# One table for the order of all steps up to the second mixture pass, the borders between the passes included

## Chip, cores and metric

The kernel runs on one core of a Trainium2 chip. The metric is device microseconds of that core from launch to end; smaller is better. A time is the median of several runs, and one run is also recorded by the hardware profiler.

## What is computed

Three layers follow each other on 2304 tokens (4 batches of 576), all in 32-bit floats. The layout calls (transposes and reshapes between the layers) are cut here:

```python
def phi(x):                       # q, k: [4, 8, 576, 64], w_phi: [64, 128]
    proj = x @ w_phi
    proj = proj - max(abs(proj), axis=-1)
    return concat(exp(proj), exp(-proj))
kv, z = phi(k).T @ v, sum(phi(k))
x = (phi(q) @ kv) / (phi(q) @ z + 1e-6)          # attention, to [2304, 512]

h = maximum(x @ moe_w_in, 0)                     # [512, 2048]
x = (h * h) @ moe_w_out                          # squared-relu MLP

p = probs / (probs.sum(-1) + 1e-9)               # mixture of 4 experts
out = sum(p[:, e] * (maximum(x @ w1[e], 0) @ w2[e]) for e in range(4))
```

## The kernel before

Every large product is made three times over with operands split into a high and a low part (`split`, L78 makes the high part with a copy on ScalarE, L83 the low part with a subtraction on VectorE or GpSimd), so that the reduced-precision matmuls add up to a 32-bit result. TensorE therefore does far more matmul time than any other engine does work.

The work has four stages.

- **Attention and half of the MLP.** Sixteen objects `Pair(b, c)`, one per batch b and pair of heads c, each load q, k and v, transpose them (`t_pe`, L203), split them (`t_hi`, `t_lo`), project them (`project`, L231 to L233), subtract the row maximum (`shift`: a reduction L239 into `mx` and a subtraction L243 into `pm`), take exponentials (`exp_k`, L256, into `kf`; `q_pe` L264 and `q_exp` L273 into `q`), multiply keys by values (`kv_pe`, L279 and L284, with `va` the values), multiply queries by that (`num_pe`, L302, with `z` the result of `kv_pe`), divide and transpose back. Batches 0 and 1 go at once into the MLP (`Unit`: `hidden` L451, `relu`, `square`, `g_hi`, `g_lo`, `out` L497, `add` L505), whose 16 weight blocks (`Matrix`) are read here as 64-bit numbers and narrowed to 32 bits in several VectorE and ScalarE steps (`widen`, L392, takes two bit masks; then `widen_power` to `widen_mul`) and stored for later.
- **MLP of batches 2 and 3** (L1128 onward): 8 groups of two weight blocks. The two batches are multiplied together in a Strassen-like scheme: `PairUnit.product` (L1029) makes seven products of six matmuls each into four accumulators `px`, `py`, `pz`, `pv`, and `PairUnit.add` (L1039) adds them into `u` on VectorE. The operands of the products (`Operands`) are B11, T2, T1, T3, B22, B21 and T4, quarters of the activations or sums of them (`f`), each with a high part `oh` and a low part `ol`. The last 64 rows of each batch are carried apart (`RestUnit.hidden`, 24 matmuls, L1059, with the operand `rest`). `Act` makes relu, square (L995, L997) and the split `gh`, `gl`; the second matmul is `MlpOut.mm` (L1082) with `MlpOut.add` (L1089).
- **Mixture of batches 0 and 1**: 16 groups of 42 product matmuls and 48 output matmuls (`MixOut.mm`, L1104, with `MixOut.add`, L1113).
- **Mixture of batches 2 and 3 and of the rest rows**: 16 groups, with `RestUnit` again.

Between two stages lies a border: the operands of the next stage are made from sums that the stage before is still finishing, and weights of the next stage are loaded, summed (`Weights.sums`, GpSimd, L932, into `f`) and split.

What runs when is an order written by hand. Each engine executes its instructions in program order, and the DMA queue of SyncE issues loads and stores in program order. The program is the list `plan`, sorted by a number. The function `at` gives each step that number: for the early part of the program, as a place out of the table `PLACES`, and after that, as a time that the formulas in `plan_tail` and its helpers work out from fixed offsets (`plan_weights`, `plan_pair`, `plan_out`, `plan_operands`):

```python
def at(t, fn, *args):
    if t < UNTIL:
        x = getattr(fn, "__self__", None)
        t = UNTIL * next(places["" if x is None else type(x).__name__, fn.__name__]) / STEPS
    plan.append((t, len(plan), fn, args))
```

Before, `UNTIL` is 485.0, and the table holds 1519 places, the attention stage and the first border. The second border (MLP to mixture) and the third (mixture to mixture with rest rows) come from the formulas.

Of the kernel before, what the change touches and what calls it, by code (L numbers as in the profile page):

```python
# [21 lines left out]
def fused_kernel(  # L22
# [484 lines left out]
    def new_x2(b):  # L507
# [12 lines left out]
            5, 8, 28,  # L520
        ),
        ("", "load_wd"): (
            1,
        ),
        ("", "split"): (
            7,
        ),
        ("Pair", "lqk"): (
            0, 12, 4, 13, 14, 29, 65, 72, 40, 104, 95, 96, 141, 117, 132, 157, 183, 218, 193, 211, 223, 285,
            300, 264, 342, 344, 308, 382, 375, 446, 451, 475, 484, 573, 549, 566, 503, 572, 529, 706, 749, 800,  # L530
            826, 924, 868, 927, 1092, 1034,
        ),
        ("Pair", "lv"): (
            18, 24, 23, 38, 33, 61, 37, 130, 133, 116, 112, 91, 152, 240, 174, 214, 187, 269, 301, 216, 338,
            362, 328, 390, 404, 318, 351, 402, 568, 464, 571, 461, 651, 643, 526, 745, 587, 825, 702, 969, 982,
            818, 1024, 771, 801, 947, 893, 1064,
        ),
        ("Pair", "t_pe"): (
            2, 6, 20, 26, 48, 41, 85, 75, 100, 127, 155, 134, 161, 171, 184, 232, 246, 216, 257, 293, 275, 311,
            340, 326, 387, 359, 410, 430, 471, 497, 534, 548, 531, 602, 654, 687, 715, 762, 780, 876, 897, 908,  # L540
            951, 962, 1008, 1009, 1072, 1105,
        ),
        ("Pair", "t_hi"): (
            3, 9, 21, 27, 54, 49, 89, 78, 114, 138, 162, 151, 173, 186, 207, 233, 254, 229, 266, 302, 278, 323,
            345, 337, 393, 388, 425, 455, 476, 510, 540, 575, 537, 607, 655, 711, 748, 768, 787, 896, 906, 920,
            955, 963, 1010, 1028, 1081, 1116,
        ),
        ("Pair", "t_lo"): (
            10, 15, 25, 36, 55, 53, 97, 90, 122, 143, 165, 154, 178, 190, 210, 241, 255, 237, 271, 310, 303,
            327, 347, 341, 395, 400, 427, 459, 487, 518, 551, 579, 557, 614, 670, 714, 750, 786, 806, 899, 932,  # L550
            948, 956, 981, 1011, 1051, 1088, 1131,
        ),
        ("Pair", "project"): (
            16, 22, 34, 51, 56, 63, 102, 99, 124, 145, 169, 170, 197, 206, 222, 249, 265, 272, 289, 313, 324,
            343, 354, 360, 405, 403, 429, 465, 506, 533, 556, 592, 623, 650, 689, 740, 778, 802, 851, 911, 944,
            959, 975, 1003, 1060, 1100, 1143, 1170,
        ),
        ("Pair", "shift"): (
            17, 30, 44, 57, 71, 79, 107, 105, 139, 149, 172, 180, 200, 225, 230, 261, 268, 283, 305, 315, 329,
            350, 358, 380, 414, 407, 443, 481, 521, 543, 588, 604, 635, 677, 707, 752, 790, 809, 862, 917, 945,  # L560
            971, 994, 1047, 1074, 1113, 1158, 1183,
        ),
        ("Pair", "exp_k"): (
            42, 32, 47, 68, 81, 84, 131, 118, 140, 179, 199, 189, 219, 227, 248, 270, 273, 297, 312, 316, 330,
            367, 368, 391, 437, 440, 457, 536, 542, 558, 615, 657, 671, 696, 712, 764, 850, 833, 869, 931, 993,
            1002, 1059, 1083, 1093, 1160, 1165, 1200,
        ),
        ("Pair", "q_pe"): (
            35, 39, 58, 64, 82, 94, 126, 119, 142, 175, 196, 198, 220, 253, 245, 286, 277, 291, 331, 320, 348,
            370, 369, 389, 428, 424, 478, 514, 581, 584, 613, 669, 675, 743, 804, 777, 835, 881, 936, 968, 990,  # L570
            1043, 1032, 1066, 1087, 1147, 1182, 1219,
        ),
        ("Pair", "q_exp"): (
            46, 50, 70, 73, 86, 111, 137, 125, 150, 182, 202, 203, 221, 262, 256, 292, 290, 299, 333, 321, 357,
            377, 383, 413, 436, 450, 483, 523, 595, 596, 634, 701, 679, 755, 836, 779, 855, 889, 939, 970, 1006,
            1044, 1041, 1068, 1115, 1180, 1189, 1223,
        ),
# [3 lines left out]
        ("Pair", "z_out"): (  # L581
            59, 93, 156, 217, 259, 307, 353, 406, 460, 587, 705, 828, 902, 1037, 1111, 1237,
        ),
        ("Pair", "num_pe"): (
            60, 74, 108, 115, 160, 176, 224, 236, 279, 267, 334, 314, 356, 376, 418, 438, 470, 490, 598, 617,
            710, 717, 839, 837, 921, 973, 1045, 1049, 1135, 1120, 1246, 1242,
        ),
        ("Pair", "den"): (
            69, 77, 113, 120, 164, 188, 228, 238, 287, 276, 335, 322, 409, 379, 419, 448, 499, 493, 599, 629,
            724, 725, 858, 848, 954, 986, 1055, 1050, 1138, 1126, 1260, 1247,  # L590
        ),
        ("Pair", "divide"): (
            83, 80, 146, 144, 208, 191, 239, 247, 295, 294, 349, 336, 411, 394, 421, 449, 504, 507, 608, 632,
            736, 731, 859, 853, 966, 991, 1061, 1057, 1145, 1139, 1261, 1251,
        ),
        ("Pair", "xt_pe"): (
            109, 153, 226, 258, 306, 355, 415, 462, 508, 641, 753, 860, 992, 1063, 1150, 1274,
        ),
        ("Pair", "x_hi"): (
            121, 163, 244, 274, 309, 361, 416, 472,  # L600
        ),
        ("Pair", "x_lo"): (
            129, 166, 250, 281, 317, 365, 417, 477,
        ),
        ("Pair", "x_rest"): (
            128, 159, 235, 263, 319, 378, 422, 463, 513, 649, 763, 879, 998, 1096, 1168, 1282,
        ),
        ("Pair", "put_rest"): (
            204, 234, 260, 346, 381, 445, 432, 625, 515, 703, 842, 1076, 1151, 1319, 1265, 1309,
        ),  # L610
        ("Pair", "x_out"): (
            527, 648, 757, 884, 1001, 1071, 1169, 1278,
        ),
        ("Pair", "put_x"): (
            726, 658, 840, 976, 1015, 1272, 1245, 1286,
        ),
        ("Matrix", "load"): (
            11, 31, 135, 106, 282, 384, 325, 442, 528, 576, 453, 662, 603, 735, 694, 751, 794, 852, 827, 886,
            957, 999, 907, 1082, 1102, 1128, 1058, 1192, 1175, 1238, 1204, 1254,
        ),  # L620
# [12 lines left out]
        ("Matrix", "widen_add"): (
            67, 103, 231, 213, 433, 435, 371, 524, 597, 656, 546, 719, 645, 773, 747, 814, 843, 903, 874, 952,
            995, 1035, 978, 1099, 1134, 1162, 1124, 1222, 1194, 1257, 1243, 1308,
        ),
        ("Matrix", "widen_sign"): (
            76, 123, 243, 252, 401, 447, 373, 525, 577, 653, 561, 722, 647, 775, 734, 824, 831, 887, 873, 949,
            1005, 1039, 961, 1090, 1133, 1176, 1107, 1224, 1201, 1270, 1234, 1304,
        ),  # L640
        ("Matrix", "widen_mul"): (
            87, 147, 280, 284, 468, 454, 386, 554, 605, 666, 590, 737, 663, 781, 783, 841, 854, 915, 877, 958,
            1022, 1054, 1007, 1108, 1140, 1178, 1132, 1225, 1232, 1279, 1255, 1312,
        ),
        ("Matrix", "store"): (
            181, 158, 372, 408, 559, 467, 486, 578, 665, 682, 591, 738, 716, 792, 817, 846, 861, 923, 922, 984,
            1038, 1077, 1018, 1144, 1159, 1185, 1220, 1249, 1331, 1292, 1275, 1346,
        ),
        ("Matrix", "hi"): (
            110, 167, 296, 304, 496, 473, 516, 609, 636, 668, 620, 744, 676, 784, 791, 864, 882, 916, 894, 996,  # L650
            1052, 1070, 1026, 1146, 1163, 1186, 1179, 1240, 1235, 1287, 1264, 1315,
        ),
        ("Matrix", "lo"): (
            185, 194, 364, 374, 502, 489, 532, 612, 652, 690, 621, 746, 767, 796, 795, 866, 885, 930, 919, 1014,
            1053, 1078, 1027, 1149, 1174, 1187, 1198, 1244, 1262, 1291, 1271, 1338,
        ),
        ("Unit", "hidden"): (
# [4 lines left out]
        ),  # L662
        ("Unit", "relu"): (
            412, 439, 501, 488, 555, 585, 611, 639, 688, 685, 759, 733, 812, 830, 898, 871, 912, 967, 1021, 989,
            1086, 1091, 1136, 1122, 1196, 1208, 1236, 1268, 1295, 1307, 1317, 1337,
# [24 lines left out]
        ),  # L690
        ("", "open_early"): (
            1322,
        ),
        ("", "open_late"): (
            1376,
# [83 lines left out]
    UNTIL = 485.0  # L779
# [490 lines left out]
```

## Time and profile before

| quantity | value |
|---|---|
| median of 3 runs | 1392.85 us (1389.75 to 1393.58) |
| time of the profiled execution | 1391.17 us |
| its span in the trace | 1389.4 us |
| TensorE (PE) busy | 1361.9 us, 98% of the span |
| VectorE (DVE) busy | 868.8 us, 63% |
| ScalarE (ACT) busy | 511.7 us, 37% |
| GpSimd (POOL) busy | 522.3 us, 38% |
| 16 DMA engines, mean | 66 GB/s to and from HBM |
| mean granted TensorE clock | 0.998 of full speed |

Busy time is the time in which an engine has an instruction under way. The profiled execution's own time is 1.8 us longer than its span, which is what lies around the recorded instructions, and 1.7 us under the median. In the profile, PE is TensorE's matmul and PEld its weight load, which overlaps it; L12 is line 12 of the kernel; a wait names the operation that the engine waited for. The four stages differ in what waits, so stretches of time are read apart: attention runs to about 395 us, the first border to 480, the MLP's middle groups to 590, the second border to 660, the first mixture's middle groups to 935, the third border to 985, and the last stage to the end.

### The profile page before, as it was taken

The numbers are of one execution on the slowest core, as the hardware profiler recorded it, in microseconds if no ns is written. First come the engines' busy times: TensorE is split into PE (matmuls) and PEld (weight loads), VectorE is DVE, ScalarE is ACT, GpSimd is POOL, SyncE is SP. The second block draws the span as 40 slices with busy tenths as digits, with TensorE's granted clock in tenths as the row PEclk, the third lists the DMA queues.
The fourth block names the chain that finished last, engine by engine and source line by source line (L and its number), as shares of the span: only waits on it lengthen the run. The fifth ranks groups of instructions, "written<-read, shape, count | busy, mean of one in ns | idle before, by whom it ended". The sixth has DMA issues, their size and how long they took to land.

```text
span 1389.4 us, 18889 instructions
## 1 busy us (share of the span) xinstructions
PE 1361.9 (98%) x7300; PEld 1171.7 (84%) x7300; DVE 868.8 (63%) x1302; ACT 511.7 (37%) x908; POOL 522.3 (38%) x382
## 2 busy tenths in 40 slices
PE   7999999999999999999999999999999999999998
PEld 7999888889877888887888888887888888888887
DVE  5777667796785455576655655668655555555554
ACT  4655655554554432342322232234312212212311
POOL 1000111110247776567544535444543443443430
PEclk9999999999999999999999999999999999999999
DMA  5433433442342111102111121213211211110102
GB/s 145 102 89 99 105 107 98 119 117 79 121 149 76 46 31 46 32 16 76 62 58 34 61 61 31 61 31 107 75 31 31 61 31 31 61 31 31 46 1 76
DMA packets 130250, 92.57 MB, mean 67 GB/s; under 512 B 65648, under 2 KB 108784, under 8 KB 130160
## 3 DMA queue, kind: packets, MB, share of 16 engines
q1 hardware_dynamic: 128848, 89.00, 22.1%
q10 hardware_dynamic: 1312, 2.36, 0.4%
q8 instruction: 58, 0.95, 0.3%
q14 instruction: 32, 0.26, 0.1%
HBM read 75.60 MB, written 15.73 MB: 66 GB/s over the span
## 4 chain that ended last, share of the span: by engine, by line
PE 92%; DVE 4%; ACT 1%; POOL 0%; DMA 0%; issue 0%; SPq 0%; ACTq 0%; DVEq 0%; POOLq 0%
PE pa L1104 27%; PE pv L1029 7%; PE pz L1029 7%; PE pa L1082 7%; PE px L1029 7%; PE pm L497 6%; PE ph L451 6%; PE pa L1059 5%; PE py L1029 4%; PE pa L302 3%; PE pa L284 2%; PE pm L302 2%; PE pm L284 2%; PE pp L231 1%; PE pp L233 1%; PE pp L232 1%
## 5 line engine op out<-in xcount | busy, mean ns | idle before, releaser
L83 POOL TENSOR_TENSOR w<-f,w 128x1024 fp32r<-128x1024 f32 (+1 forms) x80 | 184.5, 2327 | 284.3 <-ACT w L78 284.3
L1113 DVE SCALAR_TENSOR_TENSOR x<-pa,prob,x 128x512 f32<-128x512 f32 x270 | 201.8, 750 | 131.7 <-PE pa L1104 131.6
L1104 PE MATMUL pa<-w2l,gh 128*128 128x512 f32 x576 | 224.5, 390 | 1.3 <-ACT gh L1001 0.7
L1104 PE MATMUL pa<-w2h,gl 128*128 128x512 f32 x576 | 224.3, 389 | 1.0 <-DVE gl L1007 1.0
L1104 PE MATMUL pa<-w2h,gh 128*128 128x512 f32 x576 | 224.3, 389 | 0.0
L1036 ACT ACTIVATE u<-px 128x512 f32<-128x512 f32 x40 | 24.0, 599 | 455.2 <-PE px L1029 454.9
L83 POOL TENSOR_TENSOR wl<-wf,wh 128x512 fp32r<-128x512 f32 x32 | 42.7, 1338 | 346.3 <-ACT wh L78 311.7
L83 POOL TENSOR_TENSOR w2l<-f,w2h 128x1024 fp32r<-128x1024 f32 x40 | 97.1, 2428 | 137.6 <-ACT w2h L78 137.6
L1001 ACT ACTIVATE gh<-u 128x512 fp32r<-128x512 f32 x136 | 85.7, 631 | 156.2 <-DVE u L1039 149.8
L1104 PEld LDWEIGHTS pa<-w2h,gl 128*128 128x128 f32 x576 | 108.1, 188 | 24.2 <-DVE gl L1007 1.8
L1104 PEld LDWEIGHTS pa<-w2l,gh 128*128 128x128 f32 x576 | 108.2, 188 | 24.1 <-issue 1.1
L1104 PEld LDWEIGHTS pa<-w2h,gh 128*128 128x128 f32 x576 | 108.2, 188 | 21.8
L932 POOL TENSOR_TENSOR f<-f 128x256 f32<-128x256 f32 x160 | 120.2, 772 | 10.2 <-DMA f<-w_i 6.8
L1029 PE MATMUL px<-oh,w 128*128 128x512 f32 x320 | 98.6, 389 | 0.0
L1029 PE MATMUL pz<-oh,w 128*128 128x512 f32 x320 | 98.6, 389 | 0.0
L1029 PE MATMUL pv<-oh,w 128*128 128x512 f32 x320 | 98.6, 389 | 0.0
L1007 DVE SCALAR_TENSOR_TENSOR gl<-u,gh 128x512 fp32r<-128x512 f32 x96 | 73.5, 774 | 26.9 <-ACT gh L1001 25.3
L1039 DVE TENSOR_TENSOR u<-pz,u 128x512 f32<-128x512 f32 x80 | 55.3, 691 | 51.3 <-PE pz L1029 50.5
L78 ACT ACTIVATE w<-f 128x1024 fp32r<-128x1024 f32 (+1 forms) x80 | 77.1, 1009 | 6.4 <-POOL f L932 6.4
L1039 DVE TENSOR_TENSOR u<-py,u 128x512 f32<-128x512 f32 x40 | 27.7, 691 | 80.5 <-PE py L1029 50.5
L1059 PEld LDWEIGHTS pa<-rest,w 128*128 128x128 f32 x576 | 72.2, 191 | 1.8
L1089 DVE TENSOR_TENSOR x<-pa,x 128x512 f32<-128x512 f32 (+1 forms) x84 | 49.3, 600 | 37.7 <-PE pa L1082 37.6
(145 smaller groups left out, 2969.9 us busy)
## 6 DMA issues: line engine op xcount, KB each, us to landing
f<-in_moe_w_dram SPq DMA_DIRECT2D x96, 256.0 KB
raw<-in_moe_w_in_dram SPq DMA_DIRECT2D x16, 512.0 KB
raw<-in_moe_w_out_dram SPq DMA_DIRECT2D x16, 512.0 KB
f<-in_moe_w_dram SPq DMA_DIRECT2D x64, 128.0 KB
qk<-in_q_dram SPq DMA_DIRECT2D x32, 128.0 KB
qk<-in_k_dram SPq DMA_DIRECT2D x32, 128.0 KB
va<-in_v_dram SPq DMA_DIRECT2D x32, 128.0 KB
w_o<-wf SPq DMA_DIRECT2D x16, 256.0 KB
```

The costliest lines, as they stand in the source:

```text
L78: nc.scalar.activation(out=dst, in_=src, func=AF.Copy)
L83: eng.tensor_tensor(out=dst, in0=a, in1=b, op=ALU.subtract)
L451: nc.tensor.matmul(p[:, :n], lhsT=a, rhs=m, start=i == 0, stop=i == len(ops) - 1)
L497: nc.tensor.matmul(p[:, :n], lhsT=a, rhs=m, start=i == 0, stop=i == len(ops) - 1)
L932: nc.gpsimd.tensor_tensor(out=s[:, i], in0=a, in1=b, op=op)
L1001: nc.scalar.activation(out=self.gh, in_=self.r, func=AF.Copy if self.square else AF.Relu)
L1029: nc.tensor.matmul(p, lhsT=a, rhs=m, start=start and i == 0, stop=i == len(ops) - 1, skip_group_check=not start)
L1039: nc.vector.tensor_tensor(out=self.u[out], in0=self.p[a], in1=self.u[b], op=ALU.add)
L1059: nc.tensor.matmul(q, lhsT=a[:, s, k], rhs=m[:, kk], start=kk + j == 0, stop=kk == KD - 1 and j == 2)
L1082: nc.tensor.matmul(self.p[:, :n], lhsT=a, rhs=m, start=i == 0, stop=i == len(ops) - 1)
L1104: nc.tensor.matmul(self.p, lhsT=a, rhs=m, start=i == 0, stop=i == len(ops) - 1)
L1113: nc.vector.scalar_tensor_tensor(out=o, in0=p, scalar=pe, in1=o, op0=ALU.mult, op1=ALU.add)
```

## The change

The code that makes the work is the same; every step is still there once, with the same instructions. The table `PLACES` has 2800 places in place of 1519, and `UNTIL` is 1023.0, so that the table also sets the order through the MLP pass, the first mixture pass and the first group of the second one, all three borders among it. The places in the part that had a table before are new as well. The formulas still order what comes after. Lines after the table move by 76 (L1029 becomes L1105). Cut to the entries that the text speaks of:

```diff
         ("Pair", "lv"): (
-            18, 24, 23, 38, 33, 61, 37, 130, 133, 116, 112, 91, 152, 240, 174, 214, 187, 269, 301, 216, 338,
-            362, 328, 390, 404, 318, 351, 402, 568, 464, 571, 461, 651, 643, 526, 745, 587, 825, 702, 969, 982,
-            818, 1024, 771, 801, 947, 893, 1064,
+            43, 44, 39, 84, 70, 96, 65, 34, 138, 172, 177, 194, 196, 147, 101, 203, 287, 212, 289, 310, 244, 283,
+            305, 333, 430, 387, 468, 466, 390, 460, 504, 436, 488, 505, 631, 762, 712, 824, 622, 847, 1008, 811, 842,
+            1116, 1117, 1014, 1176, 1101,
         ),
         ("Pair", "t_lo"): (
-            10, 15, 25, 36, 55, 53, 97, 90, 122, 143, 165, 154, 178, 190, 210, 241, 255, 237, 271, 310, 303,
+            7, 12, 17, 38, 47, 53, 90, 68, 95, 115, 140, 150, 156, 193, 181, 234, 229, 257, 288, 269, 303, 335, 346,
...
         ("Pair", "kv_pe"): (
-            47.25, 52, 88, 92, 140.25, 148, 215, 215.25, 248.25, 251, 297.25, 298, 339, 352, 396, 399, 457.25, 458, 568.25, 586, 671.25, 692, 764.25, 765, 888, 891, 1030, 1030.25, 1109, 1109.25, 1213, 1218,
+            46, 50, 98, 97, 139, 154, 195, 198, 247, 266, 304, 302, 347, 342, 404, 406, 475, 490, 594, 585, 670, 698,
+            786, 790, 911, 900, 1010, 1012, 1118, 1125, 1220, 1197,
         ),
...
         ("Matrix", "widen"): (
-            19, 62, 168, 195, 397, 431, 332, 491, 564, 626, 535, 697, 631, 756, 700, 808, 803, 872, 849, 933,
+            129, 27, 159, 275, 421, 414, 242, 530, 545, 643, 491, 704, 599, 749, 660, 819, 750, 895, 806, 948, 970,
...
         ("Operands", "sum"): (
-            1326, 1330, 1333, 1349,
+            1324, 1330, 1350, 1390, 1782, 1837, 1844, 1845, 2608, 2626, 2627, 2636,
         ),
...
         ("Operands", "lo"): (
-            1361, 1375, 1380, 1340, 1341, 1370, 1393,
+            1353, 1367, 1373, 1365, 1347, 1380, 1408, 1897, 1877, 1914, 1925, 1942, 1922, 1954, 2675, 2684, 2682,
+            2690, 2685, 2692, 2696,
         ),
         ("Rest", "make"): (
-            1392,
+            1392, 2631,
         ),
...
         ("RestUnit", "hidden"): (
-            1407, 1474,
+            1407, 1419, 1547, 1614, 1681, 1748, 1824, 1893, 2717, 2767,
         ),
...
+        ("MixOut", "add"): (
+            1973, 1961, 2027, 1969, 1977, 1983, 1994, 1980, 2021, 2031, 2057, 2017, 2037, 2058, 2042, 2041, 2060,
...
-    UNTIL = 485.0
+    UNTIL = 1023.0
```

Three places show what this does to the engines' order; a row with `x8` stands for eight such instructions in a row, and `x_2_4480`, `va_108` or `w_8895` are buffers with their numbers.

**Place A: TensorE in the attention stage**, where the third pair's keys times values (`kv_pe`, L279 and L284) follow its last projection (L233) and two kinds of transposes (L264 for queries, L203 for the next input). Before:

```order
L233 MATMUL pp<-wd_h,th 128x256
L264 MATMUL pa<-ident,pm 128x128 x4
L203 MATMUL pa<-ident,qk 128x128 x8
L279 MATMUL pm<-va_108,kf 128x160
L284 MATMUL pm<-va_108,kf 128x80 x8
```

With the change:

```order
L233 MATMUL pp<-wd_h,th 128x256
L264 MATMUL pa<-ident,pm 128x128 x4
L203 MATMUL pa<-ident,qk 128x128 x5
L302 MATMUL pm<-z_110,q 128x96 x8
L302 MATMUL pm<-z_110,q 128x130 x2
L264 MATMUL pa<-ident,pm 128x128 x4
L231 MATMUL pp<-wd_h,tl 128x256
L232 MATMUL pp<-wd_l,th 128x256
L233 MATMUL pp<-wd_h,th 128x256
...
L279 MATMUL pm<-va_108,kf 128x160
L284 MATMUL pm<-va_108,kf 128x80 x8
```

The second half of the previous pair's `num_pe` (L302) and a whole further projection (four times L231 to L233) now stand between the projection that the exponentials need and the matmuls that need the exponentials.

**Place B: VectorE at the first border**, around the making of `rest`, with the MLP's first groups under way (`u` are sums of accumulators, L997 a square). Before:

```order
L1039 TENSOR_TENSOR u<-py,u 128x512
L1039 TENSOR_TENSOR u<-pz,u 128x512
L83 TENSOR_TENSOR rest<-x_4_4482,rest 128x1024
L1039 TENSOR_TENSOR u<-pv,u 128x512
L1039 TENSOR_TENSOR u<-pz,u 128x512
L997 TENSOR_TENSOR u<-u 128x512 x2
```

With the change:

```order
L1115 TENSOR_TENSOR u<-py,u 128x512
L1115 TENSOR_TENSOR u<-pz,u 128x512
L83 TENSOR_TENSOR f<-x_2_4472,f 128x1024
L83 TENSOR_TENSOR rest<-x_4_4474,rest 128x1024
L1115 TENSOR_TENSOR u<-pz,u 128x512
L1115 TENSOR_TENSOR u<-pv,u 128x512
L1073 TENSOR_TENSOR u<-u 128x512 x2
```

The sum `f` (operand T4) has moved to just ahead of the low part of `rest`, and the sum from `pz` now precedes that from `pv`. On TensorE a product of the second group stands between the first group's last products, and then the first `RestUnit.hidden`.

**Place C: TensorE at the third border**, the last two products of the first group (B21 into `px`, T4 into `pv`), `RestUnit.hidden` (L1059, with `rest`) and the first output matmuls. Before:

```order
L1029 MATMUL px<-ol,w_8895 128x512
L1029 MATMUL px<-oh,w_8895 128x512 x2
...
L1029 MATMUL pv<-ol,w_8895 128x512
L1029 MATMUL pv<-oh,w_8895 128x512 x2
...
L1059 MATMUL pa<-rest,w_8895 128x256 x24
L1104 MATMUL pa<-w2l,gh 128x512
```

With the change:

```order
L1105 MATMUL px<-ol,w_8861 128x512
L1105 MATMUL px<-oh,w_8861 128x512 x2
...
L1135 MATMUL pa<-rest,w_8861 128x256 x24
L1105 MATMUL pv<-ol,w_8861 128x512
L1105 MATMUL pv<-oh,w_8861 128x512 x2
...
L1180 MATMUL pa<-w2l,gh 128x512
```

The 24 matmuls of the rest rows now stand ahead of the product with T4 in place of behind it. On POOL, ahead of these matmuls, the low parts before stood as B22, B21, then four weight sums, then T4; now the four weight sums stand between B22's low part and B21's.

## Rows read from the trace of the kernel before

**Rows 1.** The page: busy time of TensorE, and one of its costliest groups.
```profile
PE 1361.9 (98%) x7300; PEld 1171.7 (84%) x7300; DVE 868.8 (63%) x1302; ACT 511.7 (37%) x908; POOL 522.3 (38%) x382
...
L1104 PE MATMUL pa<-w2h,gh 128*128 128x512 f32 x576 | 224.3, 389 | 0.0
```

**Rows 2.** Busy time by stretch (columns in the second line; x is instructions).
```profile
core 0: us, PE busy (x) PEld busy (x) DVE busy (x) ACT busy (x) POOL busy (x), PEclk, DMA share, GB/s
0.00:25.00 25.00, 18.17 (x138) 17.22 (x139) 13.79 (x22) 10.57 (x22) 4.86 (x22) 1.00 0.58 141
25.00:395.00 370.00, 364.92 (x2507) 333.46 (x2506) 270.75 (x470) 200.20 (x458) 40.58 (x31) 1.00 0.38 105
395.00:480.00 85.00, 80.15 (x392) 66.26 (x391) 52.14 (x72) 41.72 (x64) 59.45 (x39) 1.00 0.28 90
590.00:660.00 70.00, 66.80 (x338) 56.22 (x337) 49.16 (x64) 26.41 (x39) 50.57 (x33) 1.00 0.15 46
935.00:985.00 50.00, 46.94 (x215) 37.98 (x214) 41.27 (x47) 20.35 (x26) 30.38 (x19) 1.00 0.32 103
```

**Rows 3.** Waits of TensorE from 25 to 395 us: total, times, longest.
```profile
PE pa L284 <- DMA va<-in_v_dram: 1.6, 1, 1.6
PE pa L284 <- ACT kf L256: 1.3, 1, 1.3
PE pm L284 <- ACT kf L256: 0.8, 1, 0.8
```

**Rows 4.** The same from 395 to 480 us.
```profile
PE pv L1029 <- DVE u L1039: 1.3, 1, 1.3
PE pm L497 <- DVE x L505: 1.2, 1, 1.2
```

**Rows 5.** The same from 590 to 660 us.
```profile
PE pa L1082 <- DVE x L1089: 2.2, 2, 1.7
```

**Rows 6.** The same from 935 to 985 us.
```profile
PE pv L1029 <- POOL ol L83: 1.7, 1, 1.7
PE pa L1104 <- ACT gh L1001: 0.7, 1, 0.7
```

**Rows 7.** Busy time by stretch, around a wait at 201.6 us.
```profile
203.00:207.00 4.00, 4.00 (x14) 3.24 (x13) 1.77 (x2) 0.92 (x2) 0.00 (x0) 0.58 0.45 133
```

**Rows 8.** The chain that ended last (start, duration, what).
```profile
27.46 2.23 PE pm L302 x20
...
427.90 2.34 DVE rest L83
...
968.78 2.40 POOL ol L83
...
978.11 2.87 PE pa L1059 x24
...
1371.28 13.64 PE pa L1104 x60
```

**Rows 9.** Groups of instructions of VectorE by line (busy us, mean ns).
```profile
L1039 DVE TENSOR_TENSOR u<-pz,u 128x512 f32<-128x512 f32 x80 | 55.3, 691 | 51.3 <-PE pz L1029 50.5 <-POOL f L932 0.7
...
L243 DVE TENSOR_TENSOR pm<-pp,mx 128x1024 f32<-128x1024 f32 x32 | 39.2, 1225 | 5.0 <-PE pa L264 2.2 <-ACT wh L78 0.8
L239 DVE TENSOR_REDUCE mx<-pp 128x8 f32<-128x1024 f32 x32 | 39.0, 1219 | 8.8 <-PE pp L233 8.6
...
L392 DVE TENSOR_SCALAR power<-raw 128x512 uint32<-128x512 uint32 x32 | 14.9, 465 | 0.8 <-DMA raw<-in_moe_w_in_dram 0.8
```

**Rows 10.** The same of ScalarE.
```profile
L256 ACT ACTIVATE kf<-pm 128x512 f32<-128x512 f32 x64 | 36.8, 630 | 4.8 <-DVE pm L243 4.7
```

**Rows 11.** Timeline of VectorE and of POOL at the third border (start, duration, instruction).
```profile
957.76 2.42 POOL L83 TENSOR_TENSOR w2l<-f,w2h 128x1024 fp32r<-128x1024 f32 x1 [5.96 <-ACT w2h L78]
...
958.69 2.57 DVE L83 TENSOR_TENSOR ol<-x,oh 128x1024 fp32r<-128x1024 f32 x1
...
961.84 1.21 DVE L83 TENSOR_TENSOR ol<-f,oh 128x1024 fp32r<-128x1024 f32 x1
```

More of the change, by code (lines that the diff above doesn't have):

```diff
@@ L519, in fused_kernel @@
         ("", "clear"): (
-            5, 8, 28,
+            10, 57, 30,
         ),
         ("", "load_wd"): (
-            1,
+            3,
         ),
         ("", "split"): (
-            7,
+            4,
         ),
         ("Pair", "lqk"): (
-            0, 12, 4, 13, 14, 29, 65, 72, 40, 104, 95, 96, 141, 117, 132, 157, 183, 218, 193, 211, 223, 285,
-            300, 264, 342, 344, 308, 382, 375, 446, 451, 475, 484, 573, 549, 566, 503, 572, 529, 706, 749, 800,
-            826, 924, 868, 927, 1092, 1034,
+            0, 13, 5, 6, 31, 18, 42, 48, 55, 75, 110, 74, 117, 132, 165, 207, 160, 146, 243, 256, 228, 274, 246, 293,
@@ L677, in fused_kernel @@
-            1017, 1123, 1121, 1172, 1156, 1206, 1217, 1258, 1277, 1310, 1318, 1332, 1350,
+            443, 471, 501, 528, 553, 627, 611, 662, 717, 696, 793, 744, 828, 836, 897, 898, 1013, 972, 1087, 1026,
+            1114, 1090, 1181, 1151, 1230, 1223, 1260, 1277, 1306, 1331, 1337, 1345,
         ),
         ("Unit", "out"): (
[4 rows of a table removed]
[4 rows of a table added]
         ),
         ("Unit", "add"): (
[4 rows of a table removed]
[4 rows of a table added]
         ),
         ("", "open_early"): (
-            1322,
+            1318,
         ),
         ("", "open_late"): (
-            1376,
+            1383,
@@ L720, in fused_kernel @@
+            2298, 2344, 2390, 2436, 2482, 2528, 2544, 2592, 2673, 2756, 2772,
         ),
         ("Weights", "load2"): (
-            1385, 1419, 1424,
+            1358, 1397, 1447, 1537, 1604, 1671, 1738, 1806, 1908, 1912, 1953, 2025, 2096, 2142, 2188, 2234, 2280,
+            2326, 2372, 2418, 2464, 2510, 2567, 2541, 2641, 2697, 2654,
         ),
         ("Weights", "sums"): (
-            1334, 1390, 1460,
+            1320, 1369, 1475, 1521, 1588, 1655, 1722, 1781, 1854, 1960, 1997, 2024, 2079, 2125, 2171, 2217, 2263,
@@ L726, in fused_kernel @@
+            2309, 2355, 2401, 2447, 2493, 2539, 2565, 2632, 2689, 2757,
         ),
         ("Weights", "hi"): (
-            1352, 1391, 1475,
+            1326, 1394, 1482, 1524, 1591, 1658, 1725, 1783, 1849, 1964, 1966, 2033, 2082, 2128, 2174, 2220, 2266,
+            2312, 2358, 2404, 2450, 2496, 2545, 2588, 2630, 2691, 2771,
         ),
         ("Weights", "lo"): (
-            1355, 1396, 1502,
+            1327, 1396, 1507, 1527, 1594, 1661, 1728, 1804, 1880, 1974, 1990, 2047, 2085, 2131, 2177, 2223, 2269,
@@ L732, in fused_kernel @@
+            2315, 2361, 2407, 2453, 2499, 2561, 2598, 2637, 2698, 2783,
         ),
         ("Weights", "hi_sums"): (
-            1368, 1401, 1503,
+            1354, 1384, 1515, 1530, 1597, 1664, 1731, 1789, 1855, 1981, 2003, 2029, 2088, 2134, 2180, 2226, 2272,
+            2318, 2364, 2410, 2456, 2502, 2542, 2576, 2640, 2705, 2759,
         ),
         ("Weights", "lo_sums"): (
-            1374, 1411, 1504,
+            1355, 1391, 1516, 1563, 1630, 1697, 1764, 1805, 1856, 1986, 2019, 2035, 2092, 2138, 2184, 2230, 2276,
@@ L738, in fused_kernel @@
+            2322, 2368, 2414, 2460, 2506, 2547, 2599, 2647, 2708, 2760,
         ),
         ("Weights", "hi2"): (
-            1389, 1449, 1510,
+            1377, 1449, 1485, 1553, 1620, 1687, 1754, 1807, 1915, 1985, 2030, 2062, 2108, 2154, 2200, 2246, 2292,
+            2338, 2384, 2430, 2476, 2522, 2573, 2590, 2648, 2724, 2750,
         ),
         ("Weights", "lo2"): (
-            1397, 1467, 1511,
+            1411, 1450, 1497, 1568, 1635, 1702, 1769, 1852, 1917, 2002, 2032, 2063, 2109, 2155, 2201, 2247, 2293,
@@ L775, in fused_kernel @@
-            1515, 1518, 1516, 1512, 1506, 1494, 1501,
[6 rows of a table added]
+        ),
[10 rows of a table added]
+        ),
+        ("MixOut", "add"): (
[9 rows of a table added]
         ),
```

157 lines of the change are left out of this document (79 added, 78 removed), and 87 rows, old and new, of the table PLACES.

## The prediction

> **What bounds the kernel now.** I read the page first: TensorE is busy 1361.9 of 1389.4 us [rows 1]. The change leaves every instruction in place, so the most that it can win is what TensorE doesn't use, 27.5 us, and what a wait costs beside its idle time. Then the busy time by stretch, to see where these 27.5 us lie: 6.8 in the first 25 us, 5.1 in the attention stage after that (370.00 less 364.92), 4.85 at the first border, 3.2 at the second, 3.06 at the third [rows 2]; the rest (4.5) is the end, which the change does not touch. The middle groups of the passes have no idle time at all, and the change keeps their pattern. So it is an affair of the start, of a handful of waits in attention, and of three borders. Then the waits of TensorE by stretch, to see who is late: single waits, each for another operation, the exponentials `kf` and a load of `va` in attention [rows 3], sums `u` and `x` on VectorE at the first border [rows 4], `x` at the second [rows 5], a low part `ol` on POOL and `gh` at the third [rows 6]. No engine is short over a whole stretch: in attention VectorE works 271 of 370 us, ScalarE 200; at the third border VectorE works 41 of 50 [rows 2], the tightest of all. Waits of that kind are what a better order removes: something was made too late although its engine had time before.
>
> **What a wait costs.** A matmul that ends ahead of a wait is recorded with 389 ns [rows 1], while sixty in a row take 13.64 us, 0.227 each [rows 8]. So the restart adds 0.16 us to the idle time of each wait. And once a wait costs the clock: right after the one at 201.6 us the granted clock is 0.58 for 4 us [rows 7], close to the lower level of 1.2 GHz, where the stretch as a whole shows 1.00 [rows 2], the level of 2.4. Lost there: 0.42 x 4 = 1.7 us.
>
> **The change, part by part.**
> *Attention, 25 to 395 us: 5.1.* Place A shows the pattern. The matmuls of `kv_pe` need the projection reduced, shifted and put through the exponential: 1.22 + 1.23 + 0.63 = 3.1 us [rows 9, 10]. TensorE covered that with transposes and waited 0.8 [rows 3]. With the change, the second half of a `num_pe` and a whole projection stand between. The first is 2.23 us (recorded as 20 pieces) [rows 8]; the second is 12 matmuls of 256 columns, of which 24 take 2.87 us [rows 8], so 1.43. Together 3.7 against the 0.96 us that were missing: the wait goes, with 2.7 to spare. The load of `va` that was waited for 1.6 us [rows 3] was a load of the tenth pair whose place, 568, was right ahead of its use at 568.25; now that pair's loads stand at 466, 390 and 460 and its use at 585. I take all five waits of this stretch as gone.
> *First border: 4.85, six waits.* The 1.2 us wait for `x` [rows 4] came from operand subtractions standing in a row ahead of the sums; single sums now alternate with them. Place B is where something new can be late. From the end of the product into `pz`, VectorE has a sum (0.69 [rows 9]), `f` and `rest`: with `f` at 1.21 like an uncontended operand subtraction of the same size [rows 11] and `rest` at 2.34 [rows 8] that is 4.24 us. TensorE has three products meanwhile, 18 matmuls, 4.09 us. So `RestUnit.hidden` waits 0.15 us at least; if `f` is stretched as the row of 2.57 us [rows 11] is, 1.5. I take 0.4, near the low end, because most subtractions of that size are not stretched.
> *Second border: 3.2, three waits.* Two of them are sums `x` behind the operand subtractions [rows 5]; the same cure as at the first border, with no new product ahead of its operand. I take them as gone.
> *Third border: 3.06, three waits.* Place C: the wait of 1.7 us was for the low part of T4, the last thing that POOL made [rows 6]. Now the 24 matmuls of the rest rows, 2.87 us [rows 8], run ahead of T4's product and cover it. The other two, for `gh` and for a sum, are 0.7 [rows 6] and 0.6 us, each behind an operand subtraction on VectorE that now stands elsewhere; I take them as gone. In exchange the four weight sums stand ahead of B21's low part on POOL. The sums take about as long as the hidden matmuls, one subtraction is 2.40 us [rows 8]. If the sums start late, `px` waits: between 0 and 0.9 us (the 2.87 us by which B21's low part moves back, less the 1.4 of the product and 0.6 of the sum that stood between B21's and T4's need before). I take 0.5.
> *Start: 0.6.* `widen`'s masks of the first weight block stood on VectorE ahead of the low part of the second projection's input; the masks take 0.465 us [rows 9] and about as much again for the second one, and now come behind it. Bounds: 0 (another operand is late there anyway; the 6.8 us of idle time there [rows 2] are several waits) and 0.9. I take 0.6.
> *New waits of the attention stage.* Some forty places were exchanged, and the spare time that I find at the tightest is a few tenths of a us. One short wait: 0.5, between 0 and the 1.6 of the largest one that this stage shows now [rows 3].
> *Port of SBUF.* A subtraction on VectorE of 1024 columns took 1.21 us when POOL was idle and 2.57 while POOL was in a subtraction of its own from 957.76 to 960.18 [rows 11]: it cost 1.36 more. Both borders with many operands have such pairs before and after. I take half of one more collision, 0.7; it could be none, or four.
>
> **The sum.** Idle time that goes: 5.1 + 4.85 + 3.2 + 3.06 = 16.2. Restarts: 17 waits of 0.16 = 2.8 (five, six, three and three by stretch). The clock: 1.7. Together 20.7. The start: 0.6. New: 0.4 + 0.5 + 0.5 + 0.7 + three restarts of 0.16 = 2.6. From the profiled execution's own time: 1391.17 - 20.7 - 0.6 + 2.6 = 1372.5. That execution is 1.7 us under the median of the runs; from the median it would be 1374.2. I take 1373.0.
>
> **The rivals.**
> *First, the collisions decide (1378).* The new order packs operand subtractions of VectorE and of POOL closely at borders 1 and 3. With two such collisions at each, all on the path, 4 x 1.36 = 5.4 come on top: 1378. For it speaks that VectorE is the fullest engine there; against it, that before, with as many subtractions, only the few rows named above are stretched. The Trainium skill, page "SBUF — State Buffer", section "Who interferes with whom", says that a VectorE instruction with two inputs from SBUF contends with a GpSimd instruction that reads SBUF, and that the one that comes first blocks the other wholly; by that rule every overlap costs up to a whole subtraction, and the trace's 2.57 beside 1.21 us agrees in kind.
> *Second, loads come late (1381).* In the new table five of the sixteen pairs (the second, third, fourth, fourteenth and fifteenth) have their last load of `va` within two places of its use; in the old one two had (the seventh and tenth), and one of those two waited. If all five wait as that one did, 1.6 + 0.16 each, 8.7 us come back: 1381. Against it: the place orders instructions, it doesn't time them; a load needs only its buffer, and with three buffers for `va` that is free some two pairs ahead, so it is late only if something ahead of it in the queue of SyncE waits.
> *Third, slower (1400).* The same mechanism with its other end: one store that waits for its data blocks all loads behind it in SyncE's queue. If that made every pair late by 1.74 us, 28 us would be added to 1373: 1400. It decides from the eleventh late pair on, since eleven eat the gain. Against it: DMA engines are busy 0.38 of the attention stretch [rows 2] and only one wait there is for a DMA [rows 3].
> *Fourth, nothing happens (1391).* The late operations could be late because of their own inputs, whatever the order, and each wait just turn up one instruction further on. For it speaks that no engine but TensorE is full; that is also against it, since a late operation behind idle time of its own engine would be waiting for TensorE itself, and rows 4 to 6 show VectorE and POOL instead.
>
> **How the numbers follow.** The forecast (1368 to 1376) has a chance of 0.62, the collisions 0.20, the loads 0.10, slower 0.04, nothing 0.04. A measurement of this kernel can tell about 0.3%, 4.2 us. The first three are faster by more than that: 0.92; same 0.04, slower 0.04. The range: low end without any new wait and from the fastest run, 1389.75 - 21.3 = 1368.4; high end the loads' 1381.
>
> **What the changed profile would show.** Idle time of TensorE between 25 and 985 us, now 16.2, should be under 3; no granted clock of 0.58 near 200 us. At the first border the wait before `RestUnit.hidden` (L1135) should name `rest` on VectorE and be 0.15 to 1.5 us. At the third no wait for `ol` at `pv`, and at most 0.9 us at `px`. If VectorE's `ol` and `f` rows of 1024 columns average well over 1.6 us at the borders, the first rival is right; if waits for `va` appear at several pairs, the second or third. I am wrong if waits of another kind fill the same stretches.

## The result and the profile after

The change takes 1380.16 us in the median (1379.18 to 1380.25), the kernel before, run beside it, 1391.96. The ratio is 0.9915, with a 95% interval of 0.9897 to 0.9932. That is 11.8 us faster, inside the range, but 7 us slower than the 1373.0 forecast and 4 us above the 1368 to 1376 to which the forecast gave a chance of 0.62. The profiled execution took 1380.25 us with a span of 1378.4, which stands against 1391.17 and 1389.4 before.

The busy time by stretch answers to [rows 2]; the borders lie up to 10 us earlier now, so the stretches are cut anew.

```profile
0.00:25.00 25.00, 19.40 (x141) 17.99 (x142) 14.01 (x22) 11.49 (x25) 4.80 (x22) 1.00 0.61 142
25.00:390.00 365.00, 365.00 (x2519) 334.69 (x2519) 282.98 (x478) 201.70 (x459) 44.08 (x35) 1.00 0.39 110
390.00:470.00 80.00, 76.84 (x380) 63.98 (x379) 54.64 (x64) 40.87 (x61) 55.85 (x35) 1.00 0.25 80
...
580.00:650.00 70.00, 69.05 (x348) 58.37 (x347) 49.34 (x63) 27.78 (x39) 46.97 (x32) 1.00 0.15 46
...
925.00:975.00 50.00, 48.48 (x222) 39.30 (x222) 39.91 (x46) 18.15 (x23) 26.84 (x17) 1.00 0.33 106
975.00:1378.40 403.40, 397.05 (x1912) 335.11 (x1910) 222.45 (x308) 94.40 (x132) 137.53 (x94) 1.00 0.13 40
```

Read from the first two numbers of each row: TensorE's idle time went from 6.83 to 5.60 us at the start, from 5.08 to 0 in the attention stage, from 4.85 to 3.16 at the first border, from 3.20 to 0.95 at the second, from 3.06 to 1.52 at the third. After it, where the change was expected to do nothing, it rose from 4.50 to 6.35. Together that is 9.9 us less; eleven waits fewer behind the first 25 us (six in place of 17), at 0.16 each for the restart, make it 11.7, against 11.0 in the span.

The waits of TensorE in these stretches, in the same order (first border, second, third, and 975 to 1000 us), show that none of the waits of [rows 4 to 6] is left as it was:

```profile
PE pz L1105 <- DVE x L505: 1.8, 1, 1.8
PE px L1105 <- DVE ol L83: 1.2, 1, 1.2
...
PE pz L1105 <- DVE u L1115: 1.0, 1, 1.0
...
PE pz L1105 <- DVE u L1115: 1.0, 1, 1.0
PE px L1105 <- POOL ol L83: 0.5, 1, 0.5
...
PE pa L1180 <- DVE x L1187: 1.8, 1, 1.8
```

They begin at 413.8, 417.3, 600.9, 936.4, 959.8 and 993.7 us. Five of the six are for VectorE. What it does ahead of them is in its timeline; the POOL instructions beside it are in the second group of rows (start, duration, instruction):

```profile
411.94 3.06 DVE L83 TENSOR_TENSOR ol<-x,oh 128x1024 fp32r<-128x1024 f32 x1
414.93 0.68 DVE L505 TENSOR_TENSOR x<-pm,x 128x512 f32<-128x512 f32 x1
415.53 2.80 DVE L83 TENSOR_TENSOR ol<-x,oh 128x1024 fp32r<-128x1024 f32 x1
...
595.89 3.31 DVE L83 TENSOR_TENSOR f<-x,f 128x1024 f32<-128x1024 f32 x1
...
931.53 3.26 DVE L83 TENSOR_TENSOR rest<-x,rest 128x1024 fp32r<-128x1024 f32 x1
...
990.04 4.74 DVE L1083 SCALAR_TENSOR_TENSOR gl<-u,gh 128x512 fp32r<-128x512 f32 x3
...
411.51 5.73 POOL L83 TENSOR_TENSOR w<-f,w 128x1024 fp32r<-128x1024 f32 x2 [1.17 <-ACT w L78]
...
595.65 5.26 POOL L83 TENSOR_TENSOR w<-f,w 128x1024 fp32r<-128x1024 f32 x2 [1.17 <-ACT w L78]
...
931.32 2.39 POOL L83 TENSOR_TENSOR w<-f,w 128x1024 fp32r<-128x1024 f32 x1 [6.00 <-ACT w L78]
...
988.44 2.40 POOL L83 TENSOR_TENSOR w2l<-f,w2h 128x1024 fp32r<-128x1024 f32 x1
991.81 2.42 POOL L83 TENSOR_TENSOR w<-f,w 128x1024 fp32r<-128x1024 f32 x1 [0.97 <-ACT w L78]
```

A subtraction of 1024 columns, 1.21 us when POOL is idle [rows 11], takes up to 3.31 here, and each of the four long ones lies beside a subtraction of POOL that began earlier. At 931.32 POOL begins and works to 933.71; the subtraction `rest`, which begins at 931.53, ends at 934.79, 1.08 us after POOL, so nearly all of its work was done once POOL had ended. The sum `x` at 414.93, one of whose two inputs (`pm`) lies in PSUM, keeps its 0.68 us beside the same work of POOL. Ahead of the wait at 993.7 three `gl` take 4.74 us.

The wait at 993.7 had a second price. Behind it stands this row of the busy time by stretch (the granted clock is the third number from the end):

```profile
996.00:999.00 3.00, 3.00 (x9) 2.32 (x8) 1.29 (x3) 0.00 (x0) 1.49 (x3) 0.50 0.00 0
```

Nine matmuls there were late by 1.7 us in sum against their usual distance. So this profile has no half clock at 203 us, where [rows 7] had one, and has one at 996. Whether the new order removed the one at 203 is another question (see the end).

Two theories stood against each other then. **P**: VectorE's instructions with two inputs from SBUF and GpSimd's subtractions keep each other waiting, and the new order puts them side by side. **Q**: the new order puts some steps too late by itself, and POOL has nothing to do with it. The wait names did not tell them apart.

### The profile page after: what moved, and what is told of

The parts are those of the page before. It is cut to its first block, busy times and chain, and to the rows that moved or that the text cites. A ratio compares the mean times of both kernels' runs of the same rounds, so it can differ in the third digit from the quotient of the medians.

```text
span 1378.4 us, 18841 instructions
## 1 busy us (share of the span) xinstructions
PE 1360.8 (99%) x7300; PEld 1171.7 (85%) x7300; DVE 888.4 (64%) x1302; ACT 513.9 (37%) x908; POOL 523.6 (38%) x382
## 5 line engine op out<-in xcount | busy, mean ns | idle before, releaser
L83 POOL TENSOR_TENSOR w<-f,w 128x1024 fp32r<-128x1024 f32 (+1 forms) x80 | 186.1, 2344 | 280.5 <-ACT w L78 280.5
L83 POOL TENSOR_TENSOR wl<-wf,wh 128x512 fp32r<-128x512 f32 x32 | 42.0, 1321 | 339.8 <-ACT wh L78 252.3
L83 POOL TENSOR_TENSOR w2l<-f,w2h 128x1024 fp32r<-128x1024 f32 x40 | 96.5, 2413 | 126.1 <-ACT w2h L78 126.1
L1105 PE MATMUL px<-oh,w 128*128 128x512 f32 x320 | 98.6, 389 | 0.0
L1105 PE MATMUL pv<-oh,w 128*128 128x512 f32 x320 | 98.6, 389 | 0.0
L1105 PE MATMUL pz<-oh,w 128*128 128x512 f32 x320 | 98.6, 389 | 0.0
L1083 DVE SCALAR_TENSOR_TENSOR gl<-u,gh 128x512 fp32r<-128x512 f32 x96 | 77.3, 815 | 27.3 <-ACT gh L1077 26.0
L1135 PE MATMUL pa<-rest,w 128*128 128x256 f32 x576 | 72.9, 283 | 0.0
L1115 DVE TENSOR_TENSOR u<-pv,u 128x512 f32<-128x512 f32 x80 | 55.1, 689 | 26.8 <-PE pv L1105 26.5
```

Of the source, the lines that this page charges most:

```text
L83: eng.tensor_tensor(out=dst, in0=a, in1=b, op=ALU.subtract)
L1083: nc.vector.scalar_tensor_tensor(out=self.gl, in0=self.src, scalar=0.0, in1=f32(self.gh), op0=ALU.max, op1=ALU.subtract)
L1105: nc.tensor.matmul(p, lhsT=a, rhs=m, start=start and i == 0, stop=i == len(ops) - 1, skip_group_check=not start)
L1115: nc.vector.tensor_tensor(out=self.u[out], in0=self.p[a], in1=self.u[b], op=ALU.add)
L1135: nc.tensor.matmul(q, lhsT=a[:, s, k], rhs=m[:, kk], start=kk + j == 0, stop=kk == KD - 1 and j == 2)
```

## Experiments

**Which part of the change won.** Two kernels combine the two orders: in `at`, `p` is the new table's place, `key` the pair of names that it is looked up by (the lines are shortened).

```diff
+            p = next(places[key])
-            t = UNTIL * next(places[key]) / STEPS
+            t = p - 1e6 if t < 485.0 else t                  # e1: formulas after 485
+            t = next(old[key]) - 1e6 if t < 485.0 else p - 1e5   # e2: old table first
```

> New order for the steps that had a place in the old table (attention and first border), old formulas for everything after: second and third border as before. Theory A, the rearranged second and third border gave back what they won (the trace of the change shows 5 new waits from the first border on): 1380 to 1381, the same as the change. Rival B, the second and third border each won their idle time and something else went wrong: their 3.2 + 3.06 us of idle time and six restarts of 0.16 come back, 1387.

> Old order for the steps of the old table, new order for the rest: the second and third border alone are new. Theory A: 1390 to 1392, no gain. Rival B: 1385, the 7.2 us of both borders won.

Measured: e1 1381.59 us (1380.70 to 1382.49), ratio 0.9935 with an interval of 0.9920 to 0.9949; e2 1391.49 against 1391.93 before, ratio 0.9999 (0.9987 to 1.0010). The expectation for theory A holds for e2; e1 lies 0.6 us above its 1380 to 1381. e1's profile has a half clock at 14 to 18 us that the change's has not, and from 25 us to the last matmul the two traces differ by 0.2 us. Nearly all that the change wins comes from the steps that had a table before; the second and third border in their new order are worth nothing alone. It isn't that nothing happens there. These are e2's waits of TensorE from 560 to 1050 us, in place of those of [rows 5, 6]:

```profile
PE pz L1368 <- DVE u L1378: 1.9, 2, 1.0
PE pa L1443 <- DVE x L1450: 1.9, 1, 1.9
PE px L1368 <- POOL ol L83: 0.5, 1, 0.5
```

Six waits of 6.3 us idle have become four of 4.3; the two restarts saved make it 2.3, and the half clock, which stands behind the wait for `x` here too, takes 1.7 of that.

**Without POOL's share.** Both orders were run with the low parts of the last three stages' weights left out: the matmuls read the high part in their place.

```diff
-                self.h, self.l = w1[:, 0], w1[:, 1]
+                self.h, self.l = w1[:, 0], w1[:, 0]
-            sub(nc.gpsimd, self.l[:, self.part], self.f[:, self.part], f32(self.h[:, self.part]))
+            pass
```

and likewise in `lo_sums` and `lo2`.

> The change without the GpSimd subtractions that make the low parts of the weights of the last three stages (the matmuls read the high part in their place, so the result leaves the low parts out); as many matmuls, DMAs and VectorE instructions. Theory P, VectorE's instructions with two inputs from SBUF and GpSimd's subtractions keep each other waiting, and the new waits come from that: the waits at 413, 417, 600, 936 and 993 us go (1.82, 1.16, 0.95, 0.98, 1.85 and five restarts of 0.16) and the half clock after the last (1.7): 1371 within 1.5; VectorE's 128x1024 subtractions are near 1.21 us but for those beside the weight sums. Rival Q, the new order itself puts steps too late and POOL has nothing to do with it: 1379 to 1380, the same waits.

> The same edit to the kernel before (the weights' low parts left out). Theory P: the subtractions stretched at 625 to 630 and at 950 and 959 us fall to 1.21, and of the borders' waits those at 626, 629 and 953 go, in part that at 431: 3 to 6 us, 1386 to 1389. Rival Q: 1391 to 1392.

Measured: e3 1370.03 us (1369.28 to 1370.72), ratio 0.9850 (0.9833 to 0.9866); e4 1389.09 (1387.79 to 1389.54), ratio 0.9979 (0.9969 to 0.9989). So these POOL instructions cost the new order some 10 us (1380.16 less 1370.03) and the old one 2.8 (1.5 to 4.3 by the interval), though both orders issue the same ones. The profiles of e3 and e4 have a half clock between 12 and 18 us that those of the change and of the kernel before have not. From 390 us on, where that plays no part, the last matmul comes 11.0 us sooner in e3 than in the change, and 4.5 us sooner in e4 than before. In e3 one wait is left from 390 to 1000 us, the one for POOL itself, the two subtractions at the first border are short, and so is the low part of the rest rows, by its group (busy, mean ns):

```profile
PE px L1105 <- POOL ol L83: 0.5, 1, 0.5
```
```profile
411.43 1.21 DVE L83 TENSOR_TENSOR ol<-x,oh 128x1024 fp32r<-128x1024 f32 x1
412.56 0.68 DVE L505 TENSOR_TENSOR x<-pm,x 128x512 f32<-128x512 f32 x1
413.16 1.21 DVE L83 TENSOR_TENSOR ol<-x,oh 128x1024 fp32r<-128x1024 f32 x1
```
```profile
L83 DVE TENSOR_TENSOR rest<-x,rest 128x1024 fp32r<-128x1024 f32 x2 | 2.4, 1216 | 0.0
```

Theory Q, 1379 to 1380 with the same waits, falls. What e4 says of the size, 2.8, is a little under the 3 to 6 expected, and of its waits one part was a miss: the waits of the second border at 626 and 629 us, which were to go, stay (0.62 and 1.68 us at 629 and 631 there). The 2.81 us subtraction ahead of the second stays too, now beside a low part of an operand on POOL, which e4 does not leave out.

**Is it the reading?** POOL was left with an instruction of as many columns, but one that only writes, or reads one input.

```diff
-            sub(nc.gpsimd, self.l2, self.f2, f32(self.h2))
+            nc.gpsimd.memset(f32(self.l2), 0.0)      # e7
+            copy(nc.gpsimd, self.l2, f32(self.h2))   # e8
```

> The change with the weights' low parts filled with zeros by GpSimd in place of subtracted (they are left out of the result): GpSimd writes as much and reads nothing. If the reading of two engines is what collides (theory P as the trace suggests): no VectorE subtraction beside such a fill is stretched, 1370 to 1371 as without the instruction. If any GpSimd work in SBUF beside VectorE collides: VectorE is held up for the length of a fill, about 1.0 us by the row of 128x800 at 0.77, and the time lies between, 1373 to 1378.

> The same with the low parts made by GpSimd as copies of the high parts (again left out of the result): one input in place of two. If one read of GpSimd is enough to collide: the waits of the change remain in part, 1373 to 1380 by the length of a copy. If only two reads collide: 1370 to 1371.

Measured: e7 1369.19 us, e8 1369.29, both like e3. The times alone don't answer, since a fill takes 0.96 us and a copy 1.05 where a subtraction takes 2.4, so there is less to meet. The rows do. In e7 two of VectorE's subtractions lie beside fills alone, and both keep their 1.21 us:

```profile
411.61 1.21 DVE L83 TENSOR_TENSOR ol<-x,oh 128x1024 fp32r<-128x1024 f32 x1
...
915.08 1.21 DVE L83 TENSOR_TENSOR f<-x 128x1024 f32<-128x1024 f32 x1
...
411.18 0.96 POOL L1022 MEMSET w<- 128x1024 f32 x1
...
915.22 0.96 POOL L1022 MEMSET w<- 128x1024 f32 x1 [4.75 <-PE px L1105]
```

In e8 the subtractions beside copies are stretched, by half a microsecond here, and the two copies take 2.81 together:

```profile
590.40 1.77 DVE L83 TENSOR_TENSOR f<-x 128x1024 f32<-128x1024 f32 x1
592.20 1.73 DVE L83 TENSOR_TENSOR f<-x,f 128x1024 f32<-128x1024 f32 x1
...
590.05 2.81 POOL L80 CAST w<-w 128x1024 fp32r<-128x1024 f32 x2 [1.16 <-ACT w L78]
```

So one read by GpSimd is enough, and writing is not. My expectation of e8, waits in part and 1373 to 1380, was a miss: the rows are stretched, but none of the five waits comes back, because the stretch is only as long as what POOL has left to do. Two subtractions beside fills are few cases. This is what the rule named in the prediction says: the Trainium skill, page "SBUF — State Buffer", section "Who interferes with whom", has the collision between VectorE's two inputs and a GpSimd instruction that reads, not one that only writes. Here the trace agrees, 1.21 beside fills and 1.73 to 3.41 beside reads in the rows shown here.

**Moving the POOL instructions away.** e5 changes places in the table alone; nothing is left out.

```diff
 ("Weights", ...): load 2756 -> 2744.2, sums 2757 -> 2744.4, hi_sums 2759 -> 2744.6,
                   lo_sums 2760 -> 2744.7, hi 2771 -> 2744.8, lo 2783 -> 2744.9
```

> The change with one move: the sums, high and low parts of the weights of the third group of the last stage stand ahead of the second half of the group before, so that GpSimd makes them at about 976 to 982 us in place of 986 to 994, where they meet three VectorE subtractions gl. Theory P: the wait of 1.85 us at 993 goes, its restart and the half clock behind it (1.7) too: 1376.5 within 1. Rival Q, the gl are late whatever POOL does: 1380.

Measured: 1376.95 us (1376.58 to 1378.11), as theory P has it. The change was not run on that chip; in the traces, from 975 us to the last matmul, e5 is 3.7 us shorter than the change. POOL makes the block at 977, and the three `gl`, which took 4.74 us, take 2.16, not far from the 1.88 that they take in e3 with POOL idle:

```profile
977.36 4.77 POOL L83 TENSOR_TENSOR w<-f,w 128x1024 fp32r<-128x1024 f32 x2 [1.17 <-ACT w L78]
...
991.70 2.16 DVE L1083 SCALAR_TENSOR_TENSOR gl<-u,gh 128x512 fp32r<-128x512 f32 x3
```

From 975 to 1010 us no wait is left, and no half clock. At the first border, which e5 does not touch, its profile has a half clock instead (see the end).

e6 adds more moves:

```diff
 ("Operands", "sum"): T4 1845 -> 1860.5 and 2636 -> 2644.5
 ("Weights", "sums"): 2689 -> 2697.5
 ("Unit", "add"):     1376 -> 1370.5
```

> The move of e5 and three kinds more: the sum for T4 behind the two sums u at the second and third border, the four weight sums behind the low parts of B21 and T4 at the third, and one sum x ahead of the low part of T1 at the first. Theory P: beside the 3.7 us of e5 the waits at 600, 936 and 959 go (0.95, 0.98, 0.54 and three restarts), and 0.6 of that at 413, which is behind one late subtraction and one sum: 1373, between 1372 and 1377, since the low parts at 959 may meet VectorE's. Rival Q: 1379 to 1381, other waits in their place.

Measured: 1377.28 us (1377.09 to 1377.58), no better than e5: the forecast of 1373, and its 1372 to 1377, was a miss. The waits at the second border and at 936 are gone, but others came. Its waits from 390 to 1000 us, and VectorE and POOL at the third border:

```profile
PE px L1105 <- DVE ol L83: 1.8, 1, 1.8
PE pa L1180 <- DVE gl L1083: 1.7, 1, 1.7
PE pz L1105 <- DVE ol L83: 1.2, 1, 1.2
PE pv L1105 <- DVE ol L83: 0.3, 1, 0.3
```
```profile
952.89 3.42 DVE L83 TENSOR_TENSOR ol<-f,oh 128x1024 fp32r<-128x1024 f32 x1
...
955.19 3.39 POOL L83 TENSOR_TENSOR ol<-f,oh 128x1024 fp32r<-128x1024 f32 x1
...
961.44 5.20 POOL L83 TENSOR_TENSOR w<-f,w 128x1024 fp32r<-128x1024 f32 x2
```

With the weight sums behind them, the low parts on POOL came to lie beside VectorE's, and the low parts of the weights beside the `gl` at 963 to 967 us. At the first border the earlier sum only passed the time from one wait to the next: 1.2 and 1.8 in place of 1.8 and 1.2.

From this, e10 keeps e5 and T4's two sums, and e11 adds, at the first border, a later start of POOL on the second weight block:

```diff
 ("Operands", "sum"): T4 1390 -> 1392.2          # e11
 ("Weights", ...): hi_sums 1384 -> 1392.5, lo_sums 1391 -> 1392.7   # e11
```

> The change as it is, on the same chip as the two runs below, to measure them against: 1380 within 1.

> e5 and one kind of move out of e6: the sum for T4 behind the two sums u at the second and the third border, and nothing else. Theory P: the waits at 600 and 936 go beside that at 993 and no new one comes, since no GpSimd instruction is moved to where VectorE works: 2.2 us under e5, 1374.5 within 1 if the change is at 1380. Rival Q: 1377 or more, other waits in their place as in e6.

> e10 and, at the first border, the high and low parts of the second weight block's sums behind the high part of the rest rows on ScalarE, so that GpSimd starts on them at about 414 in place of 411.5 us, after VectorE has begun the low parts of T1 and B21; and the sum for T4 behind the low part of the rest rows. Theory P: the waits at 413 and 417 (1.82 and 1.16) shrink to about 0.9 together, 2 us under e10, 1372.5 within 1.2. Rival Q: no gain, 1374.5 or more, or a new wait of the second block's first product for its weights.

Measured on one chip: e9 1380.29 us, e10 1374.97 (1374.37 to 1375.72), e11 1373.30 (1372.96 to 1374.49), ratio of e11 to before 0.9868 (0.9853 to 0.9883). Both lie within their forecasts, 1374.5 within 1 and 1372.5 within 1.2. e11 beats both kernels, with every instruction of theirs. In e10 the waits at 600, 936 and 993 us are gone and no new one has come; from 390 to 1000 us it waits for

```profile
PE pz L1105 <- DVE x L505: 1.9, 1, 1.9
PE px L1105 <- DVE ol L83: 1.1, 1, 1.1
PE px L1105 <- POOL ol L83: 0.5, 1, 0.5
```

In e11, at the first border, VectorE's first subtraction starts before POOL's, the second at the same time but for 0.02 us, and neither is stretched:

```profile
412.75 1.21 DVE L83 TENSOR_TENSOR ol<-x,oh 128x1024 fp32r<-128x1024 f32 x1
...
414.49 1.21 DVE L83 TENSOR_TENSOR ol<-x,oh 128x1024 fp32r<-128x1024 f32 x1
...
418.97 3.41 DVE L83 TENSOR_TENSOR f<-x,f 128x1024 f32<-128x1024 f32 x1
...
414.47 6.83 POOL L83 TENSOR_TENSOR w<-f,w 128x1024 fp32r<-128x1024 f32 x2 [3.32 <-ACT w L78]
```

POOL pays now (6.83 for two), and so do the low part of `rest` (2.04) and T4's sum at 418.97; the waits at 413 and 417 are gone, and one of 0.92 us for POOL's low part of T4 stands in their place, with two of 0.2 us, one of them for the second block's weights, which the rival had named. By the traces, 1.1 of the 1.9 us between e10's and e11's spans are won at the border; most of the rest is at the start, which neither edit touches (see the end).

## Why the prediction was right, and where a term was off

The sign and the mechanism of the gain were right. The predicted time was 7 us too low, and the step that failed is the term "Port of SBUF". That the range held is in part luck: its high end, 1381, was the price of late loads, of which there were none, and 1380.16 lies nearer to that rival's 1381 and to the collisions' 1378 than to the forecast.

- *Attention, 5.1 us and the clock's 1.7.* Right for the 5.1: no idle time from 25 to 390 us, and no wait for a load, so neither rival about loads has anything to stand on. (Its count of five pairs leaves out the first, with 44 ahead of 46.) e1 shows that the gain lies in the steps of the first table. The clock's 1.7 is in this pair of profiles, but it is not shown to be the order's: e2 has the old order there, with the same wait, and no half clock behind it. As much was lost at 996 us, behind a wait that the prediction had not seen.
- *New waits of the attention stage, 0.5.* None came.
- *Start, 0.6.* It won 1.23 of idle time, beyond the upper bound of 0.9. Which edit did it was not tried.
- *First border.* `RestUnit.hidden` was to wait 0.4 and doesn't, in e3 neither, where no product ahead of it waits. The 2.34 us that the sum took for `rest` was itself a stretched row; alone it takes 1.22 (e3), and then the three products cover it. What was late instead were two of those products, by 1.82 and 1.16.
- *Second border, "I take them as gone".* The three waits went. One of 0.95 came, for `u` behind the sum `f` at 595.89, which took 3.31 us.
- *Third border.* The cover by the 24 matmuls worked: no wait at `pv`. The wait at `px` was put at 0.5 and is 0.54, the one new wait that has its own cause and is left in e3. The one at 936.4 was not foreseen, and neither was 993.7, behind the border.
- *Port of SBUF, 0.7.* This is the mis-sized term. The five waits that go with the instructions (1.82, 1.16, 0.95, 0.98 and 1.85), their restarts and the clock behind the last come to 9.3 us, and leaving the instructions out takes 10 us off. So the term was 8.6 too low by these waits; the waits for `rest` and in attention and the start, 1.9 together with their restarts, went the other way, which leaves 6.7 of the 7. The first rival had the mechanism, and gave it 5.4 and a chance of 0.20. Two things made it small. Its price was 1.36, from one row; a meeting costs what is left of POOL's instruction, up to 2.1 here for the sum at 595.89 (3.31 less 1.21). And the argument against it, that only a few subtractions were stretched before with as many of them, was an argument about the old order alone: e4 and e3 show that the same instructions cost 2.8 there and 10.1 here. It was a misreading of the old order too. At the three borders of the kernel before, ten of VectorE's 27 instructions of L83 with 1024 columns take more than 1.5 us; two that [rows 8, 11] don't show are

```profile
627.20 2.81 DVE L83 TENSOR_TENSOR ol<-f,oh 128x1024 fp32r<-128x1024 f32 x1
...
950.02 2.85 DVE L83 TENSOR_TENSOR rest<-x,rest 128x1024 fp32r<-128x1024 f32 x1
```

With the change they are eleven of 26, but the time beyond 1.21 us each grows from 9.1 to 15.5 us. The term also counted only subtractions of 1024 columns, where three `gl` of 512 columns made the dearest wait.

- *The fourth rival, nothing happens,* holds for the second and third border (e2, ratio 0.9999), though not by its mechanism: new waits came from another cause.
- *The signs.* Idle time from 25 to 975 us is 5.63 us where "under 3" was expected. The sign for the first rival, `ol` and `f` rows well over 1.6 us in the mean, came true at the first and second border (1.92 and 2.01) and not at the third (1.28). It was a blunt one, since the kernel before has 1.43, 1.63 and 1.44.

## What to carry to other kernels

When an order is arranged anew, list for each border which VectorE instructions read two operands from SBUF and which GpSimd instructions read SBUF beside them: a sum of durations taken from a trace with another order leaves out what they do to each other. Starting an engine a few us earlier or later can then be worth a good part of what the order on TensorE is worth: steps of two weight blocks (with what ScalarE and a load do for them) and three sums on VectorE, moved, won 7.0 us (e9 against e11) with the same instructions, on top of the change's 11.8.

## What the runs showed of the hardware

The clock falls behind some waits and not behind others of equal length, and not always behind the same wait. The change's wait of 1.85 us at 993.7 is followed by 0.50 (the level of 1.2 GHz), in e9's profile too; its wait of 1.82 at 413.8 by 1.00 (2.4 GHz; both from 415 to 419 and from 419 to 423 us). In e5's profile the same wait, 1.85 there, has a granted clock of 0.57 behind it:

```profile
417.00:421.00 4.00, 3.58 (x10) 2.38 (x10) 3.90 (x4) 0.00 (x0) 1.35 (x1) 0.57 0.20 75
```

The wait of 1.27 us for `kf` that had the 0.58 of [rows 7] behind it stands in e2 and e4 as well, which keep the old order there, and the clock does not fall behind it in either (e4's falls behind another wait, of 1.88 us for `va`); e2's row is

```profile
203.00:207.00 4.00, 4.00 (x21) 3.26 (x21) 2.56 (x3) 1.09 (x2) 0.00 (x0) 1.00 0.45 135
```

So a fall in one profile is not yet a cost of the order. The times say the same: of 19 executions of the kernel before (run beside e1 to e4), six have a mean granted clock of 1.000 and take 1389.51 to 1390.09 us, and the others, at 0.996 to 0.999, take 1391.34 to 1395.39. None of the nine executions of the change (e9's among them) has 1.000, which fits a fall near 996 in each, but only two of them were profiled.

In the first 25 us it fell in some executions only: e5's and e10's profiles have a granted clock of 0.64 and 0.59 from 13.5 to 17.6 us, and the change's, e9's and e11's have 1.00, with the same instructions there. The same matmul at 25 us comes 1.2 and 1.5 us later in e5 and e10 than in the change. I had expected the start to repeat itself. Single comparisons under 2 us between profiles are therefore made by stretch here, and not by span.
